# Reordering the start of a fused attention and feed-forward kernel, beginning its granule loads at another point, and splitting its last output tile over two PSUM tiles

## The chip, the core and the metric

The kernel runs on one core of one Trainium2 chip. The metric is device time in microseconds (us). Before the change eight runs gave a median of 224.14 us (222.54 to 225.34). All profile times below are from one profiled execution on that core; times such as "at 12.2" are us from the start of its span.

## What is computed

Attention with a mask and a distance bias per head, and a two-layer feed-forward part on its output. q, k and v are 4 batches x 8 heads x 768 positions x 64. The first 8 keys are visible to every query, other keys only to the 96 queries from their own position on.

```
scores = q @ k.T / 8 - slope[h] * dist          # masked: global keys, or 0 <= rel < 96
a      = softmax(scores)
x      = (a @ v), heads side by side            # 3072 tokens x 512
h      = x @ w_in                               # 512 x 2048
g      = s * relu(h)**2 + b
out    = g @ w_out                              # 2048 x 512, float32
```

Inputs and output are float32; the kernel casts to bfloat16 for TensorE. The scale s and the offset b are applied after the last product (b as a vector, b times the column sums of w_out).

## The kernel before, in words

**Granules.** The 3072 tokens are cut into 12 granules j of 256 tokens, three to a batch. A granule passes through these steps, each one a small function that issues instructions:

- Loads, all issued on POOL's queue, with a cast to bfloat16: `load_pairs` or `load_rows` for k and q (lines 86 to 105), `load_v` (107 to 114); `load_granule` is two DMAs each for k, q and v.
- Transposes of k and q, so that the head dimension lies on the partitions. Granules 0 to 2: `T_mm` on TensorE into PSUM and `T_ev`, its eviction by DVE or ACT (251 to 278). Granules 3 to 11: `XB`, four DMA transposes on SP's queue (280 to 301). Granule 0 comes as float32 by SP's queue into `raw32` and is cast by `cast` (148 to 157).
- Scores: for each of four head pairs hp, `S_mm` (353 to 371). In granules 0 and 1 the mask and bias are put in PSUM first by a matmul, `SB_mm` (343 to 351); later they are a product on DVE with the template `tmpl`. `S_post` (373 to 382) is the exponential on ACT, and that product.
- Values: `A(j, hp)` (391 to 423), matmuls with `vaug` (v with a column of ones), then a reciprocal and a product on DVE into `xn[j]`. `KO` and `VO` make shifted copies of k and v on DVE for granules that have an earlier neighbour.
- Transpose of xn to xT: `XT_half` or `XT_pe` on TensorE for granules 0 to 3, `XT_dma` (463), two DMA transposes on SP, for the later ones.
- First feed-forward product: `P1(j, fp)`, fp 0 to 7, eight matmuls of 256 columns each (483), ReLU on ACT (492), square on DVE (474, put off to the next `flush`). Piece fp needs slice fp of w_in, which eight DMAs bring in.
- Second product: `P2` in quarters of four matmuls of 512 columns (526), scaled and biased by DVE and stored by SP.

**What sets the order.** The schedule is manual: every engine executes its own instructions in the order in which the program's statements name them, from line 606 on. Waits between engines come from the tiles that instructions share. A tile of a pool is given out again when its last reader is done. PSUM is scarce: pools `scA` and `scB` for scores (one tile each), `av` and `pso` (one each), `psh` (two).

**The main loop.** `period(j)` (746 to 772), for j from 3 to 11, does the scores and values of granule j and between them runs items of a list: P1 of granule j - 1 and P2 of granules j - 1 and j - 2. At its end it issues `XT_dma(j)`, `VO(j + 1)` and `XB(j + 2)`, and then the rest of the list. Loads of granule j + 2 are issued after `A(j, 0)`. `pace(j)` (123) is what holds them there: a copy of one element of `xn[j]` on POOL, so that POOL's queue cannot pass before DVE has written it.

```
def pace(j):
    nc.gpsimd.tensor_copy(pdum[:], xn[j][0:1, 0, 0, 0:1])
```

**The end.** The last 128 rows are done by `P2_end` (596 to 599): 16 matmuls for columns 0 to 319 and 16 for columns 320 to 511, into the two halves of one PSUM tile, each followed by a DVE eviction (585) and a store (594). `idle(n)` (224 to 233) issues n matmuls of 512 columns whose result nobody reads.

Of the kernel before, what the change touches and what calls it, by code (L numbers as in the profile page):

```python
# [8 lines left out]
F32 = mybir.dt.float32  # L9
# [9 lines left out]
def kernel(  # L19
# [13 lines left out]
    nc = tc.nc  # L33
# [73 lines left out]
    def load_v(j):  # L107
        b, g = bg(j)
        for i in range(GB):
            sb = g * GB + i  # L110
            nc.gpsimd.dma_start(  # L111
                vaug[b][:, sb, :, 0:D],
                v[b, :, sb * P : (sb + 1) * P, :].rearrange("h p d -> p h d"),
            )
# [6 lines left out]
    pdum = const.tile([1, 1], BF16, name="pdum")  # L121

    def pace(j):
        nc.gpsimd.tensor_copy(pdum[:], xn[j][0:1, 0, 0, 0:1])  # L124

    def load_w_in(i, n):
        w = DF // n
        nc.gpsimd.dma_start(  # L128
            w_in_bf[:, :, i * w : (i + 1) * w], w_in_view[:, :, i * w : (i + 1) * w]
        )  # L130
# [20 lines left out]
    def cast(nm, half, eng=None):  # L151
        hs = slice(4 * half, 4 * half + 4)
        i, o = raw32[:, "kq".index(nm), hs, :], nat[nm, 0][:, hs, :]
        if eng is None:
            nc.vector.tensor_copy(o, i)
        else:
            nc.scalar.copy(o, i)
# [31 lines left out]
    load_pairs(1, "k")  # L189
    load_pairs(1, "q")  # L190
    load_w_in(0, 8)
    load_v(1)
    for i in range(1, 8):
        load_w_in(i, 8)
    load_pairs(2, "k")
    load_pairs(2, "q")
# [27 lines left out]
    def idle(n, tag="pso", cols=4 * P):  # L224
        ps = PS[tag].tile([P, 4 * P], F32, name="ps_i", tag=tag)
        for _ in range(n):
            nc.tensor.matmul(
                ps[:, 0:cols],
                lhsT=nc.const_aps.tensor(1.0, (P, P), BF16),
                rhs=nc.const_aps.tensor(1.0, (P, cols), BF16),  # L230
                start=True,
                stop=True,
            )
# [8 lines left out]
    def make_tmpl(h):  # L242
        slope = float(2.0 ** (-8.0 * (h + 1) / H))
        nc.scalar.activation(
            tmpl[:, h, :], base[:].rearrange("p a c -> p (a c)"), ACT.Exp, scale=slope
        )
# [1 line left out]

    tps = {}

    def T_mm(j, half, nm, tag="psh"):
        a = 0 if nm == "k" else 1
        if (j, half) not in tps:
            tps[j, half] = PS[tag].tile([P, 2, 2, GT], BF16, name="ps_t", tag=tag)
        ps = tps[j, half]
        for e in range(2):
            hp = 2 * half + e
            for i in range(GB):
                for hi in range(2):
                    nc.tensor.transpose(  # L260
                        ps[hi * D : (hi + 1) * D, a, e, i * P : (i + 1) * P],
                        nat[nm, j][:, 2 * hp + hi, i * D : (i + 1) * D],
                        ident[:],
                    )

    def T_ev(j, half, nm, eng=None):
        b, g = bg(j)
        a = 0 if nm == "k" else 1
        if j not in qT:
            qT[j] = qtp.tile([P, HP, GT], BF16, name="qT", tag="qT")  # L270
        src = tps[j, half][:, a, :, :].rearrange("p e (i t) -> p e t i", i=GB)
        hs = slice(2 * half, 2 * half + 2)
        dst = kT[b][:, hs, g * GT : (g + 1) * GT] if nm == "k" else qT[j][:, hs, :]
        dst = dst.rearrange("p e (t i) -> p e t i", i=GB)
        if eng is None:
            nc.vector.tensor_copy(dst, src)  # L276
        else:
            nc.scalar.copy(dst, src)
# [64 lines left out]
    def SB_mm(j, hp, which=None):  # L343
        ps = sc_tile(j, hp, which)
        n = ncols(j)
        c0 = 0 if n == 3 * P else P
        m = base[:].rearrange("p a c -> p (a c)")[:, c0 : c0 + n]
        for hi in range(2):
            nc.tensor.matmul(  # L349
                ps[:, hi, 0:n], lhsT=diag[:, 2 * hp + hi, :], rhs=m, start=True, stop=False  # L350
            )

    def S_mm(j, hp, biased=False, which=None):
        b, g = bg(j)
        ps = sps[j, hp] if biased else sc_tile(j, hp, which)
        own = [(kT[b][:, hp, (g * GB + i) * P : (g * GB + i + 1) * P], i) for i in range(GB)]
        if g == 0:
            plan = [own[0] + (0,), own[1] + (1,), (own[0][0], 1, 2)]
        else:
            ko = kos[j]  # L360
            plan = [own[0] + (0,), own[1] + (3,), (ko[:, hp, 0, :], 0, 1), (ko[:, hp, 1, :], 1, 2)]
        for n_, (kt, i, oc) in enumerate(plan):
            for hi in range(2):
                r = slice(hi * D, (hi + 1) * D)
                nc.tensor.matmul(  # L365
                    ps[:, hi, oc * P : (oc + 1) * P],
                    lhsT=kt[r, :],
                    rhs=qT[j][r, hp, i * P : (i + 1) * P],
                    start=not biased,
                    stop=not biased or n_ == len(plan) - 1,  # L370
                )
# [201 lines left out]
    def P2_cols(j, tb, ps, lo, hi):  # L573
        b, g = bg(j)
        flush()
        for fc in range(FC):
            nc.tensor.matmul(  # L577
                ps[:, 0 : hi - lo],
                lhsT=gT[j][:, fc, tb * P : (tb + 1) * P],
                rhs=w_out_bf[:, fc, lo:hi],  # L580
                start=(fc == 0),
                stop=(fc == FC - 1),
            )
        o_sb = work.tile([P, hi - lo], F32, name="o_sb", tag="o_sb", bufs=5)
        nc.vector.scalar_tensor_tensor(  # L585
            out=o_sb[:],
            in0=ps[:, 0 : hi - lo],
            scalar=s_bc[:],
            in1=bvec[:, lo:hi],
            op0=ALU.mult,  # L590
            op1=ALU.add,
        )
        t0 = b * S + g * GT + tb * P
        nc.sync.dma_start(out[t0 : t0 + P, lo:hi], o_sb[:])

    def P2_end(j, tb):
        ps = ps_b.tile([P, 2, DM], F32, name="ps_2e", tag="scB")
        P2_cols(j, tb, ps[:, 0, :], 0, 320)
        P2_cols(j, tb, ps[:, 1, :], 320, DM)

    def P2_sc(j, tb, which):
        pool, tag = ((ps_a, "scA"), (ps_b, "scB"))[which]
        po[j, tb] = pool.tile([P, 2, DM], F32, name="ps_2s", tag=tag)[:, 0, :]


    idle(7)
    SB_mm(0, 0)
    SB_mm(0, 1)
    cast("k", 0)
    T_mm(0, 0, "k")  # L610
    T_ev(0, 0, "k")
    cast("q", 0, "act")
    idle(2)
    T_mm(0, 0, "q")
    T_ev(0, 0, "q", "act")
    cast("k", 1)
    idle(1)
    T_mm(0, 1, "k")
    T_ev(0, 1, "k")
    cast("q", 1)  # L620
    idle(1)
    for hp in range(2):
        S_mm(0, hp, True)
        S_post(0, hp, True)
    T_mm(0, 1, "q")
    T_ev(0, 1, "q")
    more_loads()
    SB_mm(0, 2)
    S_mm(0, 2, True)
    S_post(0, 2, True)  # L630
    SB_mm(0, 3)
    S_mm(0, 3, True)
    S_post(0, 3, True)
    A(0, 0)
    A(0, 1, "pso")
    A(0, 2)
    A(0, 3, "pso")
    XT_half(0, 0, "act", "av")
    T_mm(1, 0, "k")
    T_mm(1, 1, "k")  # L640
    XT_half(0, 1, "dve", "pso")
    T_ev(1, 1, "k", "act")
    T_ev(1, 0, "k")
    SB_mm(1, 0)
    SB_mm(1, 1)
    T_mm(1, 0, "q")
    T_ev(1, 0, "q", "act")
    T_mm(1, 1, "q")
    T_ev(1, 1, "q", "act")
    KO(1)  # L650
    S_mm(1, 0, True)
    S_post(1, 0, True)
    S_mm(1, 1, True)
    S_post(1, 1, True)
    P1(0, 0)
    SB_mm(1, 2)
    S_mm(1, 2, True)
    S_post(1, 2, True)
    VO(1)
    A(1, 0)  # L660
    SB_mm(1, 3)
    S_mm(1, 3, True)
    S_post(1, 3, True)
    P1(0, 1)
    A(1, 1, "pso")
    make_tmpl(0)
    make_tmpl(1)
    A(1, 2)
    P1(0, 2)
    A(1, 3, "pso")  # L670
    P1(0, 3)
    XT_half(1, 0, "act", "av")
    XT_half(1, 1, "dve", "pso")
    P1(0, 4)
    P1(1, 0)
    P1(1, 1)
    make_tmpl(2)
    P1(1, 2)
    P1(0, 5)
    make_tmpl(3)  # L680
    P1(1, 3)
    P1(0, 6)
# [32 lines left out]
    A(2, 3)  # L715
    XB(3)
    XB(4)
    wsum_part(0)
    P2_mm(0, 0, 3)
    XT_pe(2, "act", "psh")  # L720
    wsum_part(1)
    P2_raw(0, 0)
    P2_mm(0, 1, 3)
    P2_raw(0, 1)
    wsum_part(2)
    P2_sc(1, 0, 0)
    for part in range(4):
        P2_mm(1, 0, part)
    P2_raw(1, 0)
    wsum_part(3)  # L730
    wsum_hl()
# [12 lines left out]
            P2_raw(1, 1)  # L744

    def period(j, items, at, late=None):
        SS(j, (0, 1))
        run(items, at[0])
        A(j, 0)
        if j + 2 < NJ:  # L750
            pace(j)
            load_granule(j + 2)
        run(items, at[1])
        A(j, 1)
        SS(j, (2, 3))
        if j + 1 < NJ:
            KO(j + 1)
        run(items, at[2])
        A(j, 2)
        run(items, at[3])  # L760
        A(j, 3)
        if late is None:
            XT_dma(j)
        if j + 1 < NJ:
            VO(j + 1)
        if j + 2 < NJ:
            XB(j + 2)
        if late is not None:
            run(items, 1)
            late()  # L770
            XT_pe(j, "act", "psh")
        run(items, 100)
# [80 lines left out]
```

## Time and profile before

| what | value |
|---|---|
| median of 8 runs | 224.14 us |
| the profiled execution | 223.46 us |
| its span, first to last instruction | 221.7 us |
| POOL's DMA issues, one each | 0.75 to 0.92 us |
| software DMA queue (POOL's loads) | 13.11 MB, 74.7% of 16 engines' span |
| hardware DMA queue (SP's) | 14.17 MB, 32.4% |
| P1 matmul, 256 columns | 768, mean 273 ns, 94.6 us busy |
| P2 matmul, 512 columns | 308, mean 379 ns, 78.6 us busy |
| ReLU on ACT, 128x512 | 96, mean 599 ns |
| exponential on ACT, 128x1024 and 128x768 | 48, mean 952 ns |

A group's mean duration of a matmul [...]overlaps its neighbours; what a sequence costs is read from start to start. The program shares of "busy" say how full an engine is, not what a step on it is worth; a step is worth what the work that follows it waits for. A line of the timeline gives start, duration, engine, line, operation, tiles, and in brackets the idle time of the engine before it with what released it.

### The profile page before, as it was taken

The numbers are of one execution on the slowest core, as the hardware profiler recorded it, in microseconds if no ns is written. First come the engines' busy times: TensorE is split into PE (matmuls) and PEld (weight loads), VectorE is DVE, ScalarE is ACT, GpSimd is POOL, SyncE is SP. The second block draws the span as 40 slices with busy tenths as digits, with TensorE's granted clock in tenths as the row PEclk, the third lists the DMA queues.
The fourth block names the chain that finished last, engine by engine and source line by source line (L and its number), as shares of the span: only waits on it lengthen the run. The fifth ranks groups of instructions, "written<-read, shape, count | busy, mean of one in ns | idle before, by whom it ended". The sixth has DMA issues, their size and how long they took to land.

```text
span 221.7 us, 4962 instructions
## 1 busy us (share of the span) xinstructions
PE 210.2 (95%) x1997; PEld 143.1 (65%) x2029; DVE 137.5 (62%) x321; ACT 115.4 (52%) x176; POOL 68.7 (31%) x92
## 2 busy tenths in 40 slices
PE   8869999999999999999998999999999999999992
PEld 3355887645775775775674775776666766765862
DVE  4545647679988685666675584664775765642431
ACT  6435988842764645644544635644545545542420
POOL 8657554540072450540630630630710000000000
PEclk9976999999999999999999999999999999999999
DMA  5999999999959899995899697796996131031101
GB/s 154 105 178 195 193 186 197 181 143 118 116 39 151 205 148 136 147 181 94 165 184 107 99 170 113 106 175 103 114 177 115 50 95 50 0 98 47 47 34 64
DMA packets 107208, 27.60 MB, mean 124 GB/s; under 512 B 95793, under 2 KB 104241, under 8 KB 107185
## 3 DMA queue, kind: packets, MB, share of 16 engines
q0 software_dynamic: 72896, 13.11, 74.7%
q1 hardware_dynamic: 34288, 14.17, 32.4%
q8 instruction: 16, 0.26, 0.5%
q14 instruction: 8, 0.06, 0.1%
HBM read 27.26 MB, written 6.29 MB: 151 GB/s over the span
## 4 chain that ended last, share of the span: by engine, by line
PE 86%; DMA 4%; DVE 3%; ACT 2%; issue 2%; POOL 1%; POOLq 0%; DVEq 0%; ACTq 0%
PE ps L483 37%; PE ps L526 30%; PE ps_av L410 5%; PE ps_s L365 5%; DMA vaug<-in_v_dram 4%; PE ps_2s L526 3%; PE ps_2e L577 2%; ACT pt L378 1%; PE ps_t L260 1%; PE ps_s L349 1%; DVE xn L419 1%; PE ps_x L449 1%; ACT gT L492 0%; DVE o_sb L585 0%; POOL vaug L111 0%
## 5 line engine op out<-in xcount | busy, mean ns | idle before, releaser
L483 PE MATMUL ps<-xT,w_in_bf 128*128 128x256 bf16 x768 | 94.6, 273 | 0.9 <-ACT pt L378 0.8
L492 ACT ACTIVATE gT<-ps 128x512 bf16<-128x512 f32 x96 | 57.3, 599 | 59.3 <-PE ps L483 58.4
L483 PEld LDWEIGHTS <-w_in_bf 128*128 128x128 bf16 x768 | 73.2, 98 | 18.7 <-issue 1.2
L526 PE MATMUL ps<-w_out_bf,gT 128*128 128x512 bf16 x308 | 78.6, 379 | 1.9 <-issue 0.8
L474 DVE TENSOR_TENSOR gT<-gT 128x512 bf16<-128x512 bf16 x96 | 40.1, 423 | 22.7 <-ACT gT L492 22.5
L526 PEld LDWEIGHTS <-gT 128*128 128x128 bf16 x368 | 33.6, 98 | 30.3
L378 ACT ACTIVATE pt<-ps_s 128x1024 bf16<-128x1024 f32 (+1 forms) x48 | 43.1, 952 | 19.0 <-PE ps_s L365 19.0
L382 DVE TENSOR_TENSOR pt<-pt,tmpl 128x1024 bf16<-128x1024 bf16 (+1 forms) x40 | 26.1, 652 | 13.0 <-ACT pt L378 11.9
L124 POOL COPY pdum<-xn 1x1 bf16<-1x1 bf16 x7 | 1.7, 249 | 72.9 <-DVE xn L419 72.9
L111 POOL DMA_DIRECT2D vaug<-in_v_dram x24 | 21.6, 916 | 3.6 <-DMA w_out_bf<-in_moe_w_out_dram 3.0
L419 DVE TENSOR_TENSOR xn<-ps_av,rc 128x256 bf16<-128x256 f32 x48 | 20.4, 424 | 2.1
L410 PEld LDWEIGHTS <-pt 128*128 128x128 bf16 x352 | 16.2, 99 | 8.3 <-DVE xn L419 3.0
L537 DVE SCALAR_TENSOR_TENSOR o_sb<-ps,s_bc,bvec 128x512 f32<-128x512 f32 x18 | 13.5, 748 | 12.6 <-PE ps L526 12.6
L418 DVE RECIPROCAL rc<-ps_av 128x4 f32<-128x4 f32 x48 | 8.6, 179 | 19.8 <-PE ps_av L410 19.1
L410 PE MATMUL ps_av<-vaug,pt 128*128 128x65 bf16 x224 | 17.9, 196 | 2.1 <-DMA vaug<-in_v_dram 0.8
L103 POOL DMA_DIRECT2D knat<-in_k_dram x18 | 15.8, 883 | 6.4 <-issue 2.3
L103 POOL DMA_DIRECT2D qnat<-in_q_dram x18 | 15.9, 900 | 2.1 <-DMA w_out_bf<-in_moe_w_out_dram 1.7
L365 PE MATMUL ps_s<-qT,kT 64*128 64x128 bf16 x224 | 12.7, 220 | 0.8 <-DVE qT L276 0.4
L410 PE MATMUL ps_av<-vo,pt 128*128 128x65 bf16 x128 | 12.0, 194 | 0.0
L365 PEld LDWEIGHTS <-kT 64*128 64x128 bf16 x224 | 7.2, 95 | 6.8 <-issue 6.3
L365 PE MATMUL ps_s<-qT,ko 64*128 64x128 bf16 x128 | 8.2, 219 | 0.0
L128 POOL DMA_DIRECT2D w_in_bf<-in_moe_w_in_dram x8 | 6.1, 757 | 4.5 <-DMA vaug<-in_v_dram 2.2
(66 smaller groups left out, 114.1 us busy)
## 6 DMA issues: line engine op xcount, KB each, us to landing
out_dram<-o_sb SPq DMA_DIRECT2D x23, 256.0 KB, 2.5
vaug<-in_v_dram POOLq DMA_DIRECT2D x24, 128.0 KB, 5.7
knat<-in_k_dram POOLq DMA_DIRECT2D x18, 128.0 KB, 4.5
qnat<-in_q_dram POOLq DMA_DIRECT2D x18, 128.0 KB, 4.7
w_in_bf<-in_moe_w_in_dram POOLq DMA_DIRECT2D x8, 256.0 KB, 9.8
w_out_bf<-in_moe_w_out_dram POOLq DMA_DIRECT2D x4, 512.0 KB, 13.0
raw<-in_k_dram SPq DMA_DIRECT2D x2, 256.0 KB, 3.8
raw<-in_q_dram SPq DMA_DIRECT2D x2, 256.0 KB, 4.1
```

What stands on the lines that cost most here:

```text
L103: nc.gpsimd.dma_start(t[:, i, :, :], src[b, :, sb * P : (sb + 1) * P, :].rearrange("h p d -> p h d"))
L111: nc.gpsimd.dma_start(vaug[b][:, sb, :, 0:D], v[b, :, sb * P : (sb + 1) * P, :].rearrange("h p d -> p h d"),)
L365: nc.tensor.matmul(ps[:, hi, oc * P : (oc + 1) * P], lhsT=kt[r, :], rhs=qT[j][r, hp, i * P : (i + 1) * P], start=not biased, stop=not bias ...
L378: nc.scalar.activation(pt[:, :, 0:n], ps[:, :, 0:n], ACT.Exp, scale=QSCALE)
L382: nc.vector.tensor_tensor(pt[:, :, 0:n], pt[:, :, 0:n], m, ALU.mult)
L410: nc.tensor.matmul(av[:, i, hi, :], lhsT=pt[:, hi, c * P : (c + 1) * P], rhs=vv, start=n_ == 0, stop=n_ == len(ops) - 1,)
L419: nc.vector.tensor_tensor(xn[j][:, :, 2 * hp : 2 * hp + 2, :], av[:, :, :, 0:D], rc[:].to_broadcast((P, GB, 2, D)), ALU.mult,)
L474: nc.vector.tensor_tensor(gs, gs, gs, ALU.mult)
L483: nc.tensor.matmul(ps[:, i, :], lhsT=w_in_bf[:, kc, fc * P : (fc + 1) * P], rhs=xT[j][:, kc, :], start=(kc == 0), stop=(kc == KC - 1),)
L492: nc.scalar.activation(gs, ps[:], ACT.Relu)
L526: nc.tensor.matmul(po[j, tb], lhsT=gT[j][:, fc, tb * P : (tb + 1) * P], rhs=w_out_bf[:, fc, :], start=(fc == 0), stop=(fc == FC - 1),)
L537: nc.vector.scalar_tensor_tensor(out=o_sb[:], in0=po[j, tb], scalar=s_bc[:], in1=bvec[:], op0=ALU.mult, op1=ALU.add,)
```

## The change

Line numbers here are those of the kernel before. The change has five parts.

1. **Order of the first two granules** (606 to 683). The bias matmuls of the first two head pairs go behind the first k transposes; the first scores go ahead of the second half of k. The q transposes of granule 0 get PSUM tiles of their own (`own`), and the last eviction of q is split in two. The value products of granule 0 are put between scores 2 and 3 and on, with `A(0, 3)` behind the k transposes of granule 1. P1(0, 0) goes ahead of granule 1's scores, and the later P1 pieces move up. Two of the k and q evictions of granule 1 change engines (ACT for DVE and the reverse). One `idle` matmul fewer is issued.
2. **w_in's second slice** is loaded ahead of v of granule 1.
3. **Around XT of granule 2** (718 to 731): three quarters of P2(1, 0) and two parts of the column sums (`wsum_part`) change places with P2(0, 0) and `XT_pe(2)`.
4. **Loads in the loop**: `pace` and `load_granule` stand at the top of `period(j)`, and `pace(j)` reads the last head pair of `xn[j - 1]`.
5. **The end**: the two column pieces go to tiles of two pools, `scA` and `scB`.

```diff
     def pace(j):
-        nc.gpsimd.tensor_copy(pdum[:], xn[j][0:1, 0, 0, 0:1])
+        nc.gpsimd.tensor_copy(pdum[:], xn[j - 1][0:1, 0, H - 1, 0:1])
...
     load_w_in(0, 8)
+    load_w_in(1, 8)
     load_v(1)
-    for i in range(1, 8):
+    for i in range(2, 8):
         load_w_in(i, 8)
...
-    def T_mm(j, half, nm, tag="psh"):
+    def T_mm(j, half, nm, tag="psh", own=False):
         a = 0 if nm == "k" else 1
-        if (j, half) not in tps:
+        if own or (j, half) not in tps:
             tps[j, half] = PS[tag].tile([P, 2, 2, GT], BF16, name="ps_t", tag=tag)
...
     def P2_end(j, tb):
-        ps = ps_b.tile([P, 2, DM], F32, name="ps_2e", tag="scB")
-        P2_cols(j, tb, ps[:, 0, :], 0, 320)
-        P2_cols(j, tb, ps[:, 1, :], 320, DM)
+        for pool, tag, lo, hi in ((ps_a, "scA", 0, 320), (ps_b, "scB", 320, DM)):
+            ps = pool.tile([P, 2, DM], F32, name="ps_2e", tag=tag)
+            P2_cols(j, tb, ps[:, 0, :], lo, hi)
...
-    idle(7)
-    SB_mm(0, 0)
-    SB_mm(0, 1)
+    idle(7, "av")
     cast("k", 0)
     T_mm(0, 0, "k")
     T_ev(0, 0, "k")
+    SB_mm(0, 0)
+    SB_mm(0, 1)
     cast("q", 0, "act")
-    idle(2)
-    T_mm(0, 0, "q")
+    T_mm(0, 0, "q", "pso", True)
     T_ev(0, 0, "q", "act")
     cast("k", 1)
-    idle(1)
+    idle(2, "av")
+    for hp in range(2):
+        S_mm(0, hp, True)
+        S_post(0, hp, True)
     T_mm(0, 1, "k")
     T_ev(0, 1, "k")
     cast("q", 1)
-    idle(1)
-    for hp in range(2):
-        S_mm(0, hp, True)
-        S_post(0, hp, True)
-    T_mm(0, 1, "q")
-    T_ev(0, 1, "q")
+    idle(1, "av")
+    SB_mm(0, 2)
+    T_mm(0, 1, "q", "av", True)
+    T_ev(0, 1, "q", None, (0,))
+    T_ev(0, 1, "q", None, (1,))
     more_loads()
-    SB_mm(0, 2)
+    SB_mm(0, 3)
     S_mm(0, 2, True)
     S_post(0, 2, True)
-    SB_mm(0, 3)
+    A(0, 0, "pso")
     S_mm(0, 3, True)
     S_post(0, 3, True)
-    A(0, 0)
-    A(0, 1, "pso")
-    A(0, 2)
-    A(0, 3, "pso")
-    XT_half(0, 0, "act", "av")
+    A(0, 1)
+    A(0, 2, "pso")
     T_mm(1, 0, "k")
     T_mm(1, 1, "k")
-    XT_half(0, 1, "dve", "pso")
+    T_ev(1, 0, "k", "act")
+    A(0, 3)
+    XT_half(0, 0, "act", "pso")
+    SB_mm(1, 0)
+    XT_half(0, 1, "dve", "av")
+    T_mm(1, 0, "q")
     T_ev(1, 1, "k", "act")
-    T_ev(1, 0, "k")
-    SB_mm(1, 0)
+    T_ev(1, 0, "q")
     SB_mm(1, 1)
-    T_mm(1, 0, "q")
-    T_ev(1, 0, "q", "act")
     T_mm(1, 1, "q")
     T_ev(1, 1, "q", "act")
     KO(1)
+    P1(0, 0)
     S_mm(1, 0, True)
     S_post(1, 0, True)
     S_mm(1, 1, True)
     S_post(1, 1, True)
-    P1(0, 0)
+    P1(0, 1)
     SB_mm(1, 2)
...
-    P1(0, 1)
...
     def period(j, items, at, late=None):
+        if j + 2 < NJ:
+            pace(j)
+            load_granule(j + 2)
         SS(j, (0, 1))
         run(items, at[0])
         A(j, 0)
-        if j + 2 < NJ:
-            pace(j)
-            load_granule(j + 2)
```

## The prediction

> **What bounds the kernel now.** I read the engine shares first, then TensorE's (PE's) waits, then busy time by stage, then the end and the transposes in the loop.
>
> ```profile
> span 221.7 us, 4962 instructions
> ...
> PE 210.2 (95%) x1997; PEld 143.1 (65%) x2029; DVE 137.5 (62%) x321; ACT 115.4 (52%) x176; POOL 68.7 (31%) x92
> ...
> PEclk9976999999999999999999999999999999999999
> ```
>
> PE is busy in 95% of the span, and the change leaves its real work as it is (one dummy matmul of 0.2 us fewer). So only two things can be gained: PE's idle 221.7 - 210.2 = 11.5 us, of which 3.3 lie behind its last matmul, and the slices in which its clock was reduced. PE's waits, whole kernel (columns: total us, times, longest):
>
> ```profile
> PE ps L483 <- ACT pt L378: 0.8, 1, 0.8
> PE ps_av L410 <- DMA vaug<-in_v_dram: 0.8, 2, 0.6
> ...
> PE ps_2e L577 <- DVE o_sb L585: 0.6, 1, 0.6
> PE ps_av L410 <- DVE rc L418: 0.6, 1, 0.6
> ...
> PE ps_t L260 <- DVE qnat L155: 0.5, 1, 0.5
> PE ps_s L365 <- DVE qT L276: 0.4, 1, 0.4
> ```
>
> All but the first and the third lie before 15 us. Busy us by stage (after ACT and POOL: clock, DMA share, GB/s):
>
> ```profile
> 9.80:13.25 3.45, 1.73 (x26) 1.03 (x26) 0.97 (x4) 1.55 (x3) 1.49 (x2) 1.00 1.72 165
> 13.25:16.65 3.40, 3.07 (x36) 2.43 (x38) 1.57 (x6) 1.03 (x2) 1.48 (x2) 0.51 1.92 176
> 16.65:20.06 3.41, 2.94 (x29) 1.63 (x29) 3.07 (x6) 1.18 (x3) 2.36 (x3) 0.50 1.51 194
> 20.06:26.86 6.80, 6.65 (x98) 5.21 (x96) 2.96 (x11) 6.50 (x10) 4.36 (x6) 0.99 1.51 193
> ```
>
> After a stretch with PE half idle, the clock is 0.5 from 13.3 to 20.1; then PE and ACT are both full (6.65 and 6.50 of 6.80). The end:
>
> ```profile
> 213.89 2.34 PE L577 MATMUL ps_2e<-w_out_bf,gT 128*128 128x320 bf16 x16
> 216.27 0.55 DVE L585 SCALAR_TENSOR_TENSOR o_sb<-ps_2e,s_bc,bvec 128x320 f32<-128x320 f32 x1 [1.42 <-PE ps_2e L577]
> 216.87 1.48 PE L577 MATMUL ps_2e<-w_out_bf,gT 128*128 128x192 bf16 x16 [0.64 <-DVE o_sb L585]
> ```
>
> The second column piece waits for the first one's eviction.
>
> **What the Trainium skill says.** "TensorE: Matmul & The Clock Gate", Part 1: the clock is either full or half, decided by activity in free-running windows of about 3.4 us, whose phase differs from run to run. The trace agrees: half clock for 20.06 - 13.3 = 6.8 us, two windows. "DMA: Bandwidth & Descriptors", Queues, rings and completion order: each DMA engine serves its queues in turn, packet by packet. The trace fits: an xT transpose landed after 2.4 us with no loads about (179.5) and after 3.0 to 4.6 us under the tail of a load. "PSUM — Partial Sum Buffer", PSUM bank collisions: two engines' accesses to one bank need a guard, and different banks run side by side; here even two halves of one tile are guarded, at 0.64 us. "SBUF — State Buffer", its single rule: DVE and GpSimd block each other on a shared port; the VO copy took 0.86 us while POOL issued DMAs (18.66) and 0.43 without (82.10).
>
> **Part 5, the end.** Own tiles remove the 0.64. The new tile, scA, was last used by an output tile evicted at 205.5, so nothing holds it. DVE has evicted the first piece (0.55) before the second is done (1.49). Next comes the same eviction and store. Value taken: -0.64 (bounds -0.6 and -0.7).
>
> **Part 4, loads in the loop.** POOL's trigger moves from A(j, 0) to A(j - 1, 3). In the period at 81.9: the last xn ends at 81.84 and XT is issued at 81.91; POOL's first load, now at 91.30, would come some 0.68 after xn (90.62 to 91.30 today), at 82.5, nine us sooner. Its six DMAs (0.88 each) then go by 87.8. What they newly lie beside:
> - *XT.* The second transpose goes at +1.25 from the first and lands at +3.65 if alone (1.25 + 2.4). P1 wants it at +4.9 (81.91 to 86.85; 131.25 to 136.11 and 179.52 to 184.46 give the same). Today the previous load's tail covers both; only at 114.08 did they land 4.6 and 4.4 later, the second at 119.73, with P1 starting at 119.83: this is the 0.84 that the waits put down to ACT, long done. After, the tail is gone and the load's head comes: from 62.73, data began at about 64.3 and moved at only 14 to 76 GB/s for the first 0.8 us. So the head starts at about +2.2 and is weak while the second transpose moves. I take a landing of 2.4 to 3.5: no stall. Of the old 0.84 I count -0.6, as one profile does not show how often it occurs (bounds -0.84 and 0).
> - *SP's queue.* XB's four transposes meet the load itself: at 66.4 such ones took 4.7 to 5.6 instead of 2.5. kT is read by KO some 10 us later, qT some 18 us later: covered. The stores behind them have five output buffers. XB(j + 2) finds its load long landed.
> - *DVE.* VO may go from 0.43 to 0.86 per copy, KO loses as much; DVE is at 62% and is idle 0.6 and 0.45 us right after VO: 0.
>
> In period 3 the load of granule 5 follows that of granule 4 at 48, beside the column sums, f32 sums of 1.23 us that keep DVE full from 48 to 58; if they stretch, P2 of granule 2 waits. 0 taken, +0.3 at worst.
>
> **Part 3, around XT(2).** PE idles 0.3 us in 45 to 50 in all, 0.19 of it before A(2, 3). -0.1.
>
> **Parts 1 and 2, the start.** v of granule 0, the first entry in POOL's DMA queue, lands at 12.19 both times: that is the gate. Up to it:
> - k's first transposes start at 4.7 (its cast ends at 4.64) instead of 5.13, and the bias matmuls follow. q's transposes stay at about 6.6, the first scores near 7.7 (7.94 today).
> - The cast of q's second half gets later: scores to 8.2, k transposes 0.41, eviction 0.69, cast 0.57, q transposes 0.41, half an eviction 0.4: scores of pair 2 at about 10.7 (10.15 today). Hidden by v.
> - A(0, 0) now blocks PE until 12.2, and S_mm(0, 3) is queued behind it: about 12.5 (10.86 today), its exponential done at 13.6. Only A(0, 3) needs it, and that stands behind 16 k transposes, which can start when k of granule 1 lands (4.37 + 9.2 = 13.6).
> - From 13.6 PE runs without the gaps of today (0.64, 0.19, 0.22). At half clock: transposes 1.06, A(0, 3) 0.5, XT 0.5, bias 0.86, XT 0.5, q 0.53, bias 0.86, q 0.53: 18.9, against 19.4 today.
>
> Then P1(0, 0) goes before the scores. *If the clock stays half to 20.06*, its eight matmuls take 1.7 us (to about 20.4), and ACT starts ReLU, then the exponentials: these begin at 21.05. Today they begin at 20.30 with the ReLU (0.6) still to do, so equal work is at 20.90. ACT then is full as it was: nothing gained, up to +0.2 lost. *If the clock is back at 16.65*, one window sooner, because PE has no gaps and a bias matmul in that window, the rest (XT 0.2, q 0.41, bias 0.43, q 0.41, P1 0.87) ends near 19.0 and ReLU at 19.6: 1.3 us sooner than 20.90. Which it is the trace of before can't tell: a window with 3.07 busy of transposes and short products did not restore the clock, one with 2.94 and three long bias matmuls did. With a phase that differs between runs I take the middle, -0.7 (bounds +0.2 and -1.3).
>
> Part 2: POOL's w_in(1) goes 1.7 us sooner (8.58 to 6.84), which P1(0, 1) wants at about 20; v of granule 1 comes some 2 us later, about 19; VO, the next in DVE's order, is wanted by A(1, 0) at 22: covered, and +0.5 if it is not. Slice 5 (issued 15.33, landing after 9.3 to 11.4: 24.6 to 26.7) is wanted at about 26: just covered.
>
> **Sum.** -0.7 - 0.64 - 0.6 - 0.1 = -2.0 us against the profiled 223.46 (span 221.7 and 1.8 around it), 221.5. The median is 0.7 above that execution, so 224.14 - 2.0 = **222.1**.
>
> **Rivals.**
> - *ACT takes PE's place* (0.26): ACT's 6.50 of 6.80 speaks for it, the idle PE before 15 us against. The start gives 0 and the stall at 119 recurs elsewhere: -0.64, 223.5.
> - *Slower: the load's head hits XT* (0.13). In five periods (5 to 9) XT meets a new load. It decides once the second transpose lands later than 3.65 after its issue. With the 4.4 of 114.08: 5.65 - 4.9 = 0.75 each, 3.75, less the 0.84 already paid and 1.4 gained at both ends: +1.5, 225.6; with the 5.1 of XB under a full load, 1.45 each: 229. For it: transposes share engines with loads; against: the weak first 0.8 us.
> - *The clock never drops* (0.06): PE is dense enough before 13.25. Then 2.6 at the start, -2.6 - 0.64 - 0.84 = -4.1, 220.0. Against it: PE's wait for v stays.
>
> **How the numbers follow.** Forecast 0.55, its own range 221.0 to 223.0. A difference under about 0.5% (1.1 us) can't be told from none here. Faster: 0.55 + 0.06 = 0.61; same: 0.26; slower: 0.13. The range leaves out the last rival and the larger half of the slower one: 220.5 to 225.2.
>
> **What would show it.** Right: no gap between the last two groups of matmuls; xT landing under 3.65; clock back near 16.7; the first ReLU near 19 to 20.5. Wrong: P1 waits of 0.5 us or more at the head of each period; a half clock to 20 or longer; PE gaps between 20 and 30 that end with ACT.

## The result and the profile after

The changed kernel takes 236.94 us (median of 11 runs, 232.55 to 240.51) against 224.05 us before (32 runs in the same hours): slower. The ratio is 1.048, 95% interval 1.042 to 1.054; it leaves out runs that lie over 1.5% above their kernel's fastest, and the profiled execution below, at 240.5 us, is one of the longer ones.

The shares of the engines, of the page after:

```profile
span 238.7 us, 4960 instructions
...
PE 215.1 (90%) x1996; PEld 145.4 (61%) x2028; DVE 137.0 (57%) x322; ACT 116.0 (49%) x176; POOL 70.0 (29%) x92
...
PEclk9958999999999999995899799999799999999999
```

The span grew by 17.0 us. TensorE (PE) is busy for 4.9 us more with the same work, and idle for 12.1 us more. The clock row (PEclk, tenths of full clock) tells where most of the 4.9 come from: beside the drop at the start there are now slices at 5 to 8 tenths in the second half, where before had none. PE's longest waits, whole kernel:

```profile
PE ps L486 <- DMA xT<-xn: 12.4, 5, 3.4
PE ps_av L413 <- DMA vaug<-in_v_dram: 3.0, 2, 2.4
```

P1 waits for the xT transposes in five places, 12.4 us in all (2.2, 3.4, 3.2, 1.7 and 2.0, in order of time); before, this was one wait of 0.8. The longest of them, from the timeline (start, duration, what):

```profile
100.38 2.51 SPq L466 DMA_TRANSPOSE xT<-xn  x2
100.48 0.24 POOL L124 COPY pdum<-xn 1x1 bf16<-1x1 bf16 x1 [12.58 <-DVE xn L422]
101.02 1.77 POOL L103 DMA_DIRECT2D knat<-in_k_dram  x2 [0.30 <-issue]
...
108.70 0.61 PE L486 MATMUL ps<-xT,w_in_bf 128*128 128x256 bf16 x2 [3.39 <-DMA xT<-xn]
```

The two transposes and the load of the next granule but one go off together. In the same place of the chain of work that ended last:

```profile
100.69 0.88 SPq L466
101.57 0.05 issue
101.63 7.03 DMA xT<-xn
```

The second transpose took 7.03 us to land. What this did to the clock (busy us of PE, PE load, DVE, ACT, POOL; then clock, DMA share, GB/s):

```profile
100.00:104.50 4.50, 4.45 (x30) 2.78 (x29) 2.13 (x5) 1.25 (x3) 3.72 (x6) 1.00 0.76 82
104.50:108.70 4.20, 0.81 (x14) 0.34 (x13) 1.86 (x3) 1.51 (x2) 1.78 (x3) 0.90 2.70 96
108.70:112.00 3.30, 3.08 (x11) 1.80 (x13) 0.43 (x1) 0.60 (x1) 0.00 (x0) 0.50 2.15 149
112.00:116.00 4.00, 4.00 (x26) 2.70 (x25) 0.94 (x3) 0.60 (x1) 0.00 (x0) 0.66 1.21 215
```

In 104.5 to 108.7 PE does almost nothing; then it works at half clock until about 114.7 (0.50 up to 114, 0.83 in 114 to 116). Half of these 6.0 us, some 3 us by this estimate, is lost on top of the wait of 3.4, which so is paid nearly twice. The clock did not fall behind each of the five: half clock followed the waits of 3.4, 3.2 and 2.0 us, and not those of 2.2 and 1.7.

The end went as forecast, and a little better. DVE's two last evictions of the kernel after:

```profile
234.09 0.55 DVE L588 SCALAR_TENSOR_TENSOR o_sb<-ps_2e,s_bc,bvec 128x320 f32<-128x320 f32 x1 [1.42 <-PE ps_2e L580]
...
235.41 0.42 DVE L588 SCALAR_TENSOR_TENSOR o_sb<-ps_2e,s_bc,bvec 128x192 f32<-128x192 f32 x1 [0.77 <-PE ps_2e L580]
```

The second follows the first by 1.32 us; before it was 2.12 (216.27 to 218.39), so 0.80 is gained where 0.64 was forecast.

### The profile page after: what moved, and what is told of

Its sections match the earlier page's. It is cut to its first block, busy times and chain, and to the rows that moved or that the text cites. A ratio compares the mean times of both kernels' runs of the same rounds, so it can differ in the third digit from the quotient of the medians.

```text
span 238.7 us, 4960 instructions
## 1 busy us (share of the span) xinstructions
PE 215.1 (90%) x1996; PEld 145.4 (61%) x2028; DVE 137.0 (57%) x322; ACT 116.0 (49%) x176; POOL 70.0 (29%) x92
## 4 chain that ended last, share of the span: by engine, by line
PE 73%; DMA 17%; issue 2%; ACT 2%; DVE 2%; SPq 2%; POOL 1%; POOLq 0%; ACTq 0%
PE ps L486 33%; PE ps L529 23%; DMA xT<-xn 13%; PE ps_av L413 5%; DMA vaug<-in_v_dram 4%; PE ps_s L368 4%; PE ps_2s L529 3%; SPq L466 2%; PE ps_2e L580 1%; PE ps_t L262 1%; ACT gT L495 1%; PE ps_s L352 1%; ACT pt L381 1%; DVE xn L422 1%; PE ps_x L452 1%
## 5 line engine op out<-in xcount | busy, mean ns | idle before, releaser
L486 PE MATMUL ps<-xT,w_in_bf 128*128 128x256 bf16 x768 | 98.2, 279 | 12.5 <-DMA xT<-xn 12.4
L486 PEld LDWEIGHTS <-w_in_bf 128*128 128x128 bf16 x768 | 74.8, 100 | 32.8 <-issue 11.5
L529 PE MATMUL ps<-w_out_bf,gT 128*128 128x512 bf16 x308 | 81.0, 388 | 2.1 <-issue 1.0
L529 PEld LDWEIGHTS <-gT 128*128 128x128 bf16 x368 | 34.2, 99 | 31.5 <-issue 1.7
L124 POOL COPY pdum<-xn 1x1 bf16<-1x1 bf16 x7 | 2.5, 355 | 72.5 <-DVE xn L422 72.5
L413 PEld LDWEIGHTS <-pt 128*128 128x128 bf16 x352 | 17.1, 101 | 9.6 <-issue 3.5
L413 PE MATMUL ps_av<-vaug,pt 128*128 128x65 bf16 x224 | 18.7, 201 | 3.3 <-DMA vaug<-in_v_dram 3.0
L413 PE MATMUL ps_av<-vo,pt 128*128 128x65 bf16 x128 | 12.1, 195 | 0.0
```

Source lines behind the costliest of these rows:

```text
L413: nc.tensor.matmul(av[:, i, hi, :], lhsT=pt[:, hi, c * P : (c + 1) * P], rhs=vv, start=n_ == 0, stop=n_ == len(ops) - 1,)
L486: nc.tensor.matmul(ps[:, i, :], lhsT=w_in_bf[:, kc, fc * P : (fc + 1) * P], rhs=xT[j][:, kc, :], start=(kc == 0), stop=(kc == KC - 1),)
L529: nc.tensor.matmul(po[j, tb], lhsT=gT[j][:, fc, tb * P : (tb + 1) * P], rhs=w_out_bf[:, fc, :], start=(fc == 0), stop=(fc == FC - 1),)
```

## The experiments

Theory: the load of granule j + 2 and the transposes of xT[j - 1] now meet in the DMA engines, the second transpose lands late, P1 waits, and PE's clock falls in the wait. Rivals: the changed start loses; loads that come early do harm in another way; the loss is not tied to the wait.

**Part 4 undone, and each part by itself.** The first is the changed kernel with `pace` and `load_granule` at their old place; the second is the kernel before with part 4 alone:

```diff
-        nc.gpsimd.tensor_copy(pdum[:], xn[j][0:1, 0, 0, 0:1])
+        nc.gpsimd.tensor_copy(pdum[:], xn[j - 1][0:1, 0, H - 1, 0:1])
...
+        if j + 2 < NJ:
+            pace(j)
+            load_granule(j + 2)
         SS(j, (0, 1))
         run(items, at[0])
         A(j, 0)
-        if j + 2 < NJ:
-            pace(j)
-            load_granule(j + 2)
```

> The changed kernel with part 4 undone: loads issued after A(j, 0) again, all else as changed. Theory (the load's head delays the second xT transpose, P1 waits, and the clock falls behind it): the five waits of P1 for xT (12.4 us) and the half-clock slices after 100 us are gone, time 222.5 to 224.0, that is -0.6 to -1.5 against before from the end and the start. Rival (the start loses too, since v of granule 0 landed 1.4 us later in the changed kernel): 224.5 to 226.

Measured: 222.54 us (22 runs) against 223.69 before; ratio 0.999 (0.994 to 1.003).

> The kernel before with part 4 alone. Theory: the whole loss is here, 235 to 239, P1 waits on xT in periods 5 to 9 of 10 to 14 us in sum. Rival (the stalls need the changed start or come from something else): below 230.

Measured: 239.34 us (4 runs). Its waits, and below them those of the first kernel (part 4 undone):

```profile
PE ps L483 <- DMA xT<-xn: 12.6, 5, 4.0
PE ps_av L410 <- DMA vaug<-in_v_dram: 2.3, 2, 1.8
```

```profile
PE ps_av L413 <- DMA vaug<-in_v_dram: 2.9, 2, 1.6
PE ps L486 <- DMA xT<-xn: 2.0, 1, 2.0
```

The whole loss is part 4. The changed start is no part of it: v of granule 0 landed 8.0 to 10.4 us after its issue in the eleven traces of this study, in kernels with the old start (8.5 to 10.4) and the new one (8.0 to 10.2) alike, so the late v in the trace after is within what differs from run to run.

The other parts alone; part 5 is the `P2_end` of the diff, parts 1 and 2 the order of the first two granules and w_in's second slice:

> The kernel before with part 5 alone (the last two column pieces in two pools). Expected by the sum of the prediction: -0.6, about 223.4, with no gap between the last two groups of matmuls. If the store path sets the end instead: 0.

Measured: 223.24 against 223.69, ratio 0.999 (0.995 to 1.002): too small for the runs to settle. In its trace the gap between the last two groups of matmuls is gone (one group of 32 matmuls).

> The kernel before with parts 1 and 2 alone (order of the first two granules and w_in's second slice). Prediction: -0.7, between +0.2 and -1.3. Rival, from the changed kernel's trace, where v of granule 0 landed at 13.65 instead of 12.19: 0 to +1.0.

Measured: 222.45 us (6 runs) against 223.69, ratio 0.990 (0.984 to 0.995). In its trace, the longest of the six runs (224.91), the first ReLU begins at 18.92, and the clock is 0.93 of full from 16.65 to 20.06 (0.50 before).

**When the load begins.** The changed kernel, with one line different; POOL now waits for the last element of xT[j - 1], that is for both transposes:

```diff
-        nc.gpsimd.tensor_copy(pdum[:], xn[j - 1][0:1, 0, H - 1, 0:1])
+        nc.gpsimd.tensor_copy(pdum[:], xT[j - 1][0:1, KC - 1, GT - 1 : GT])
```

> The changed kernel, but the loads of granule j + 2 wait for the last element of xT[j - 1], so they begin when both xT transposes have landed, some 3 us later than in the change and 6 us sooner than before. Theory (it is the meeting with the load's head that costs, not that loads are early): no P1 wait on xT, 221 to 222.5, at or below the changed kernel without part 4 (222.5), since the load's tail also ends before the next transposes. Rival (early loads harm in another way, by k and q transposes or stores that come late): above 226.

Measured: 220.52 us (6 runs) against 223.15 before on the same chip, ratio 0.990 (0.983 to 0.996), a little below the expected range. Its first lines of PE's waits:

```profile
PE ps L529 <- issue: 0.8, 5, 0.2
PE ps_t L262 <- DVE knat L155: 0.8, 1, 0.8
PE ps_i L228 <- PEq L839: 0.8, 1, 0.8
PE ps_av L413 <- DMA vaug<-in_v_dram: 0.6, 1, 0.6
```

No wait for xT is left. In the period at 79.65 the load begins 4.4 us after the first transpose's issue (84.05), against 0.6 in the change and some 9.4 before. So early loads are no harm; meeting the transposes is.

The same with the first transpose only (`P - 1 : P` in place of `GT - 1 : GT`):

> As the one before, but the loads wait only for the first of the two xT transposes, so that POOL issues them about 0.6 us after it lands, when the second one (which goes 1.25 us behind) is about to move or land. Theory: the load's data begin 1.6 us after that and miss the second transpose: 221 to 223. If what hurts is POOL's issuing itself and not the load's data, the second transpose lands late (over 4 us) and the time is 226 to 234.

Measured: 220.30 us (20 runs), ratio 0.991 (0.987 to 0.994), again a little below the expected range. POOL issues the first load at 83.83, while the second transpose (issued at about 82.0) is under way; it lands after 2.5 us all the same. This fits a delay by the load's data, which come later, and not by POOL's issuing; but the issuing overlaps the last 0.7 us of that transpose only, so this rival is made unlikely rather than excluded.

**The same late landing, with its wait covered.** Two quarters of P2 go ahead of P1(m, 0), loads as changed:

```diff
-            [(P1, m, 0), (P2, l, 4), (P1, m, 1), (P2, l, 5), (P1, m, 2), (P2, l, 6), (P1, m, 3), (P2, l, 7)]
+            [(P2, l, 4), (P2, l, 5), (P1, m, 0), (P2, l, 6), (P1, m, 1), (P2, l, 7), (P1, m, 2), (P1, m, 3)]
```

> The changed kernel with loads as changed, but two quarters of P2 (0.86 us each) are done ahead of P1(m, 0) in periods 4 to 11. The late landing stays, its wait is covered by 1.73 us. Theory: waits of 2.2, 3.4, 3.2, 1.7, 2.0 us shrink to 0.5, 1.7, 1.5, 0, 0.3 (12.4 to about 4), and with them most of the lost clock: 225 to 230. Rival (the loss is a lower clock or contention not tied to that wait): 233 or more.

Measured: 225.31 us (4 runs) against 223.15, ratio 1.012 (1.004 to 1.020), 11.6 below the change:

```profile
PE ps L529 <- DVE o_sb L540: 2.7, 8, 0.4
...
PE ps L486 <- DMA xT<-xn: 0.6, 1, 0.6
```

The second transposes land after 5.3 to 6.3 us here too, but the wait for them is 0.6 us; a new one appears, 2.7 us in eight periods, as P2's next output tile now waits for DVE to empty the last. Less was left of the wait than expected.

**The clock by itself.** The changed kernel with `idle(8)` after the first scores of periods 5 to 9:

```diff
         SS(j, (0, 1))
+        if 5 <= j <= 9:
+            idle(8)
         run(items, at[0])
```

> The changed kernel with 8 dummy matmuls of 512 columns (some 1.7 us) between the first scores and P1(m, 0) in periods 5 to 9, where PE waits for xT. They do no work; they keep PE active. Theory (the loss is the wait plus a clock that falls in it): the clock stays full after 20 us, the transposes land as late as ever, and the time falls by the half-clock loss alone, some 2 to 5 us, to 232 to 235. Rival (the lower clock costs nothing, the wait is all): 237 or, since the dummies take PE time, more.

Measured: 230.87 us (4 runs), ratio 1.031 (1.025 to 1.037), 6.1 below the change: work that nobody reads made the kernel faster. Busy us and clock of 20 to 180 us, of the kernel after and of this one:

```profile
20.00:180.00 160.00, 145.45 (x1380) 99.55 (x1403) 98.66 (x227) 83.42 (x123) 57.35 (x70) 0.96 1.40 130
```

```profile
20.00:180.00 160.00, 155.48 (x1473) 105.41 (x1495) 102.83 (x237) 86.39 (x128) 56.02 (x69) 1.00 1.42 136
```

The dummies hold PE for 9.5 us by their trace, with 1.7 and 0.8 us of waits before and behind them, 12.0 together, near the 12.4 of the change; the second transposes land late here too, after 5.1 to 6.1 us. What they save is the clock. In 20 to 180 us the trace after lost some 6.4 us to it (0.04 of 160), this one nothing; but the trace after is one of the longest runs. By the runs the clock's part is nearer 4: three of the four runs with dummies kept a mean clock of 0.997 or more, at the start too, which none of the change did, and the fourth (0.991) took 232.65, 4.3 below the median of the change. The expected range, 232 to 235, was a little high. That an idle PE loses the clock agrees with the Trainium skill, "TensorE: Matmul & The Clock Gate", HAM oscillation, whose rule is that PE should have no idle gaps of more than about 3.4 us. Here shorter ones could be enough. In the traces of the change, of part 4 alone, of the change without part 4 and of the start alone, half clock followed all four waits above 3 us, two of the six between 1.9 and 2.4 (1.95 and 2.36), and none of the two shorter ones.

**Transposes beside loads, measured by themselves.** SP issues two transposes of 128x512, POOL six loads or others, both released by the same DVE instruction where they are set off together; three repeats.

> A measurement by itself, which computes nothing of the reference (the output is zeros): pairs of DMA transposes of 128x512, alone (yalone); set off together with six k, q and v loads (ysix), with two v loads (ytwo), with three loads of w_in slices, whose rows are 1 KB (ywide); set off when the first of six loads has landed (ymid), or the fifth (ytail). Theory from the two traces: alone 2.4 us; ysix second one 5 to 7; ymid 4 to 6; ytail 3 to 3.7. If the size of the load's rows is what matters, ywide stays under 3.5; if the number of loads queued matters, ytwo is well under ysix.

Measured, us from issue to landing, median of three:

| beside | first | second |
|---|---|---|
| nothing | 2.5 | 2.5 |
| six k, q, v loads set off together | 2.5 | 5.3 |
| two v loads set off together | 3.4 | 4.5 |
| w_in slices set off together | 3.8 | 6.0 |
| six loads, the first landed | 5.9 | 5.7 |
| six loads, the fifth landed | 2.4 | 2.5 |

Loads with longer rows (the w_in slices) do no less harm, two loads do most of the harm of six (2.0 us of delay against 2.8), and in the middle of a load the first transpose is late as well. Only when the load is all but through is nothing left; the expected 3 to 3.7 there was wrong, since less than 1 us of load remained and a transpose's data begin to move 1.2 us after its issue (the views in the next section).

**The new load point alone**, the kernel before with the load begun when xT has landed (the two edits shown above):

> The kernel before, with its loads begun when both xT transposes have landed and nothing else changed. Theory: before, the load's tail met the transposes now and then and cost P1 some 1 to 2.4 us in a run (0.84 in the first profile, 1.0, 2.0 and 2.4 in three others), so 222 to 223, with no wait of P1 on xT. Rival (the gain of the version with all parts is the start's and the end's): no change, 223.2 or more.

Measured: 222.50 us (14 runs) against 223.93, ratio 0.996 (0.993 to 1.000); no wait for xT in its trace. This fits that before paid for the load's tail: its trace and the three others with that load point (0.8, 2.0, 1.0 and 2.4 us) each have one such wait, every time in the same period, near 120. The interval all but touches 1, so the gain is small at best.

## Why the prediction was wrong

**The step that failed** is in Part 4, XT: "the head starts at about +2.2 and is weak while the second transpose moves. I take a landing of 2.4 to 3.5: no stall." It landed after 4.9 to 7.0 us. The DMA views of the kernel after show it: busy share of the engines and GB/s in slices of 0.15 us from the first transpose's issue, first a period without a load (from 181.0), then one with it (from 161.6):

```profile
DMA  0000000059994000089993000299982000499961
GB/s 0 0 0 0 0 0 0 0 118 224 217 213 99 4 0 0 14 167 222 213 203 55 0 0 0 36 195 220 220 174 30 0 0 0 80 213 217 212 140 13
```

```profile
DMA  0000000059994005986899999999999999999999
GB/s 0 0 0 0 0 0 0 0 118 224 217 213 99 4 3 37 61 54 39 54 95 143 160 182 229 251 214 150 112 105 119 128 142 150 141 132 124 134 117 104
```

The first transpose (slices 8 to 12, counted from 0) is the same in both. The second is over in slices 16 to 21 in the period without a load; in the other the engines are 5 to 9 tenths busy from slice 15 on with 37 to 61 GB/s, and the second transpose lands only 5.5 us after its issue, in the load's body. I had read the low GB/s of a load's head as a low use of the engines. The view of before from which the 14 to 76 GB/s were read (62 to 66 us, slices of 0.1) has the busy share in the line above:

```profile
DMA  0000000000000600000000024345999999999999
GB/s 0 0 0 0 0 0 0 0 0 0 0 0 0 164 0 0 0 0 0 0 0 0 0 14 29 24 29 38 76 68 113 137 150 156 148 150 109 91 105 87
```

At 14 to 38 GB/s the engines are 2 to 5 tenths busy, and at 76 they are 9 tenths busy: the head was not weak for whoever shares these engines. I had also taken the 3.0 of transposes under a tail as their price beside any load. That the tail was mild because it ended as their data began to move fits the table above (2.5 once the fifth load has landed), but was not tested in the kernel.

Point by point:
- *The slower rival* had the mechanism, place and deciding point (3.65 after issue). Its size was wrong twice. It priced the landing at 4.4, a wait of 0.75 in each period, 3.75 in sum; measured were 12.4, about 2.5 each. And it left out the clock. Sum of the loss, from the traces of the change and of the change without part 4: the spans differ by 238.7 - 221.9 = 16.8, the waits by 12.4 - 2.0 = 10.4, and the lost clock is some 6.4 (at the start both have a clock of 0.83 in 0 to 20, and v is waited for 3.0 and 2.9). By the medians the loss is 14.4 (222.54 to 236.94), which leaves some 4 for the clock if the waits are those of the trace; the dummies give 4.3. Its upper bound, 1.45 for each period from XB's 5.1 us under a full load, still short of 2.5, was in the profile of before and was set aside; the chance of 0.13 was too low for a transfer on the path with 1.25 us of slack.
- *The old stall* of 0.84 counted as -0.6 was right in kind: 1.0 to 2.4 in other traces, and 1.4 us by the medians when the load point alone is moved to where it meets nothing. The change itself did not remove it.
- *SP's queue, VO, KO, the column sums*: 0 each; in the change PE waits for none of them. Right. The VO copies of the loop did not stretch either: each took 0.43 in 80 to 190 us.
- *Part 5*: -0.64 forecast, -0.80 in the trace between the two evictions; by the runs -0.45 and not resolved.
- *Parts 1 and 2*: -0.7 forecast as the middle of the two cases (the middle of the stated bounds, +0.2 and -1.3, would be -0.55); -1.2 by the medians, more by the ratio. The clock came back sooner in the trace of the start alone, as the better of the two cases had it. But the larger effect is one that the prediction gave 0.06: *the clock never drops*. Of the seven traces with the new start, three (both later load points, and the dummies) have full clock from 6 to 24 us, against none of the four with the old start. Every run has its mean clock on record: it was 0.997 or more in 23 of 54 runs of the four kernels with the new start and without the stalls of part 4 (start alone, change without part 4, both later load points), and in 9 of 109 runs with the old start (before, end alone, new load point alone). So the start gains, at least in part, by how often the clock stays full; why it does so in some runs only was not found. That ACT takes PE's place did not come true.
- *All parts but the fourth* come to -1.15 by the medians (222.54), against -1.4 in the sum, with an interval that holds no change. *Part 3* was not run alone.

The best version is the change with the load begun when the first xT transpose has landed, 220.30, or both, 220.52; the two can't be told apart. Both beat the kernel before by about 1%, the start and the end included.

## What to carry to other kernels

Before a transfer is moved earlier, list the short transfers on the path that it will then meet, and price them with the worst landing that the profile shows beside a full load, not beside the end of one. Read how free the DMA engines are from their busy share, not from the GB/s. If the path has less slack than that, hold the bulk transfer back with an instruction that reads what the short one wrote: one line turned a loss of 13 us into a gain of 2.6. On TensorE a wait of 2 us may, and each above 3 us here did, cost more than its length through the clock, so filling it with other work pays; here even dummies did.

## What the runs showed of the hardware

A pair of 128x512 DMA transposes lands after 2.5 us alone; beside two loads of 128 KB the second takes 4.5, beside six 5.3, beside w_in slices 6.0. The prediction's source, "DMA: Bandwidth & Descriptors", Queues, rings and completion order, fits in kind (queues served in turn). But by my estimate from the view without a load, where a transpose's data move in about 0.75 us, a fair half of the engines' time would have delayed them by as much again, not by the 2.4 to 4.5 us that the second transposes of the change show. Why the share is so small was not found.
